# Two transformer layers on one Trainium2 core: six groups of three pairs of feature tiles, with a group's block products between the second products of the group before

## The chip, the core and the metric

The kernel runs on one core of one Trainium2 chip. Its time is the device time in microseconds (us) of one execution of the whole program. Every time quoted here comes from the runs of the kernel before or from one profiled execution of it. In the profile PE is the matrix engine (TensorE), PEld its weight loads, DVE the vector engine, ACT the scalar engine, POOL GpSimd, and SP the sync engine, which in this kernel issues most of the loads.

## The reference

The input is one sequence of 2048 rows of 576 numbers. Two layers follow each other, each of them an attention over eight neighbours at distance two and a feed-forward network with SiLU, both behind a layer norm and a residual sum:

```python
# D = 576, F = 4608, H = 32 heads of 18, window W = 8, dilation 2
x = x + A(layernorm(x), wqkv, wo)
x = x + B(layernorm(x), w1, w2)
x = x + A(layernorm(x), wqkv, wo)
x = x + B(layernorm(x), w1, w2)

def B(x, w1, w2):
    h = silu(x @ w1)          # 2048 x 4608
    return h @ w2             # 2048 x 576
```

A takes, for each row s, the keys and values of the rows s, s-2, ..., s-14 (none before the first row), a softmax over these eight per head, and a projection with wo.

## The kernel before

**Stages.** The 2048 rows are cut into four chunks of 512, and the two layers give eight stages, numbered s = 0 to 7. A stage is the feed-forward network of its chunk, with the attention, the projection and the layer norm of the next stage running beside it on DVE, ACT and POOL and in between on PE (`front`, `attention`, `project`, `forms`). The hidden dimension of 4608 is cut into 36 tiles of 128. float32 values are carried as two fp16 halves, so that each product is made of three matmuls (high by high, high by low, low by high).

**The order.** Nothing is issued as it is written. Each operation goes into a list (`op`, line 79) with an engine, a duration, what it reads and writes and a priority; a small number is urgent. `Plan.order` (line 113) then runs a list schedule: whenever an engine is free in its model, it takes the ready operation of the smallest priority, and among equals the one written first. The result is a fixed order on each engine. On the chip an engine executes its list in order and waits at a semaphore where an operand is not there; everything behind it on that engine waits too.

**Stages 2 to 7** use `ffn_pairs` (line 1068). Two feature tiles and two halves of the chunk make a 2 by 2 block product, which is made from seven block products instead of eight (P1 to P7, lines 1082 to 1108). There are 18 pairs of feature tiles. For each pair:

- Seven weight tiles `wf` (160 KB each, 12 buffers, so 12 block products ahead at most) and two second-weight tiles `w2` (288 KB each, 11 buffers) are loaded by SP (lines 1015 and 856).
- Each of the seven block products is seven matmuls of 128x256 (line 1087) into one of four PSUM banks, called z0, z1, misc0 and misc1.
- ACT copies three of the sums out (L1091), DVE adds three more (L1094), ACT applies SiLU (L1110 to L1114), and ACT and DVE write the two halves of the hidden tile `h` (L1117, L1120; 5 buffers).

The pairs are taken in groups of `G2 = (5, 4, 5, 4)`. When the pairs of a group are through, `second` (line 1128) multiplies them with the second weights: for each of the four row tiles j of the chunk, the n pairs are summed in one of two accumulators `acc` (12 matmuls of 128x288 for each pair, line 1141), and DVE adds the accumulator, scaled, to the residual x (`add_to`, line 848). An `acc` bank can be written again only when DVE has done that. The scales of a group are worked out once, in `tables` (line 946).

All block products and all second products of a stage have the same priority, `pp`, so the order among them is that in which they are written, except that a block product of the next group goes first where a second product is not ready in the model.

**What else stands in the SP queue.** SP also loads the qkv weights of the attention (`wq`, 1080 KB, line 616, one buffer in these stages), x (line 1245), edges of the keys (lines 730 and 731), and issues the transposes for the layer norms (line 459) and for the seven forms of the next stage's input (`xf`, line 1062; 9 buffers, 7 used in a stage). A DMA that waits for a buffer holds all DMAs behind it in the queue.

Of the kernel before, what the change touches and what calls it, by code (L numbers as in the profile page):

```python
# [31 lines left out]
NFT = F // P  # L32
G0 = 6
NB = 2
G1 = 9
# [3 lines left out]
KH = D // 2  # L39
KB = 5 * P  # L40
LNX = 512.0
G2 = (5, 4, 5, 4)
W2N = 11
FAR = 6
PREP = 0.9
# [218 lines left out]
def sliding_attention_silu_ffn(ctx: ExitStack, tc: tile.TileContext, x, wqkv, wo, w1, w2, out):  # L264
    nc = tc.nc
    cp = ctx.enter_context(tc.tile_pool(name="const", bufs=1))
# [4 lines left out]
    op = S.op  # L271

    def fl(t):
        return t.rearrange("p a b -> p (a b)")
# [5 lines left out]
    def T(b):  # L280
        return S.tags[b.tag][b.slot]
# [87 lines left out]
    w2s = [tc.dram_tile([P, 2 * D], F16, name=f"w2s{f}") for f in range(NFT)]  # L369
# [34 lines left out]
    s12 = cp.tile([P, NFT, 2], F32, name="s12")  # L404
# [9 lines left out]
    dz = accw[:, NP:NP + NP // 2, :].rearrange("p a b -> p (a b)")  # L414
    pace = cp.tile([1, 1], F32, name="pace")
    cg = cp.tile([P, NFT // G0], F32, name="cg")
    cg4 = cp.tile([P, 4], F32, name="cg4")
    su = cp.tile([P, NU + 1], F32, name="su")
    ru = cp.tile([P, NU + 1], F32, name="ru")
    du = cp.tile([P, NU], F32, name="du")  # L420
# [43 lines left out]
    PACE_WQ, PACE_WO, PACE_W = (1, 7, 0, 6), (2, 2, 3, 3, 3), (4, 5, 6, 7)  # L464
    gate = []
    formed = []
    highs = []
    turned = []
    marks = []
# [383 lines left out]
        op("SP", 0.38, lambda: nc.sync.dma_start(fl(T(w)), w1s[f]), [("w1s", f)], [w], prio, nbytes=P * 20 * P)  # L853
        return w

    def load_w2(f, prio, kind="w2"):
        w = Buf(kind)
        op("SP", 0.38, lambda: nc.sync.dma_start(fl(T(w)), w2s[f]), [("w2s", f)], [w], prio, nbytes=P * 4 * D)
        return w

    raws = {}
# [84 lines left out]
    def tables():  # L946

        def fn():
            both = s12.rearrange("p f i -> p i f")
            n = 2 * (G2[0] + G2[1])  # L950
            for i, m, cuts in ((1, G1, ((slice(0, 4), slice(0, G1)),)),
                               (2, n, ((slice(0, 4, 2), slice(0, 2 * G2[0])), (slice(1, 4, 2), slice(2 * G2[0], n))))):
                sh, d2 = shs[i], d2s[i]
                nc.vector.scalar_tensor_tensor(sh, both[:, 0], HSH, both[:, 1], op0=ALU.mult, op1=ALU.mult)
                v, r = (t.rearrange("p (g f) -> p g f", f=m) for t in (sh, r12.rearrange("p f i -> p i f")[:, 1]))
                for g, f in cuts:
                    nc.vector.tensor_reduce(cg4[:, g], v[:, :, f], axis=AX.X, op=ALU.min)
                for g, f in cuts:
                    w = f.stop - f.start
                    nc.vector.tensor_tensor(v[:, :, f], r[:, :, f], cg4[:, g, None].to_broadcast([P, NFT // m, w]), op=ALU.mult)  # L960
                nc.vector.reciprocal(d2, cg4)
        op("DVE", 1.9, fn, [("s12", f) for f in range(NFT)], [("sh", i, g) for i in (1, 2) for g in range(4)] + ["cg4"], -0.5)

    def pair_scale():

# [102 lines left out]
    def ffn_pairs(s, xf, xs):  # L1068

        pp, pd = s + 0.5, s - 0.5  # L1070
        q0 = 0
        for g, n in enumerate(G2):
            hb, wbs = [], []
            for q in range(q0, q0 + n):
                wf = {k: load_wf(q, W_ROW[k], pd) for k in P_ORDER}
                w2b = [load_w2(2 * q + f, pd) for f in range(2)]
                c, a, b = Buf("zz"), Buf("zz"), Buf("zz")
                hq, h = Buf("hq" if s >= NC - 1 else "ha"), Buf("hp")
                hb.append(h)
                wbs.append(w2b)  # L1080

                def product(k, z, first, last, wf=wf):
                    def mm():
                        t, w, v = T(z)[:, 0:2 * P], T(wf[k]), T(xf[k])
                        pl = ((0, 0), (3, 0), (0, 3), (1, 1), (4, 1), (1, 4), (2, 2))
                        for m, (u, r) in enumerate(pl):
                            nc.tensor.matmul(t, w[:, u, :], v[:, r, :], start=first and m == 0, stop=m == 6, skip_group_check=True)  # L1087
                    op("PE", 0.763, mm, [wf[k], (xf[k], 0), (xf[k], 1)], [z], pp)

                def snap(z, r, hq=hq):  # L1090
                    op("ACT", 0.32, lambda: nc.scalar.activation(T(hq)[:, r], T(z)[:, 0:2 * P], AF.Copy), [z], [(hq, r)], pd - 0.01)  # L1091

                def add(z, r, hq=hq):
                    op("DVE", 0.36, lambda: nc.vector.tensor_tensor(T(hq)[:, r], T(z)[:, 0:2 * P], T(hq)[:, r], op=ALU.add),  # L1094
                       [z, (hq, r)], [(hq, r)], pd - 0.01)
                product("P5", c, True, False)
                product("P1", a, True, False)
                snap(c, 3)
                snap(a, 0)
                product("P3", c, False, True)  # L1100
                product("P6", a, False, False)
                product("P2", b, True, True)
                snap(a, 1)
                add(b, 0)
                add(c, 1)
                product("P7", a, False, False)
                add(a, 3)
                product("P4", a, False, True)
                d = dz[:, q:q + 1]
                op("ACT", 0.41, lambda a=a, hq=hq, d=d: nc.scalar.activation(T(hq)[:, 2], T(a)[:, 0:2 * P], AF.Silu, scale=d),  # L1110
                   [a, "wsc"], [(hq, 2)], pd - 0.01, table="silu")
                op("ACT", 0.61, lambda hq=hq, d=d: nc.scalar.activation(T(hq)[:, 0:2], T(hq)[:, 0:2], AF.Silu, scale=d),
                   [(hq, 0), (hq, 1), "wsc"], [(hq, 0), (hq, 1)], pd, table="silu")
                op("ACT", 0.41, lambda hq=hq, d=d: nc.scalar.activation(T(hq)[:, 3], T(hq)[:, 3], AF.Silu, scale=d),  # L1114
                   [(hq, 3), "wsc"], [(hq, 3)], pd, table="silu")
                sc = shs[2][:, 2 * q:2 * q + 1]
                op("ACT", 1.08, lambda hq=hq, h=h, sc=sc: nc.scalar.activation(  # L1117
                    T(h)[:, 0].rearrange("p f t -> p (f t)"), T(hq).rearrange("p r t -> p (r t)"), AF.Copy, scale=sc),
                   [(hq, r) for r in range(4)] + [("sh", 2, g)], [(h, 0)], pd)
                op("DVE", 1.2, lambda hq=hq, h=h, sc=sc: nc.vector.scalar_tensor_tensor(  # L1120
                    T(h)[:, 1].rearrange("p f t -> p (f t)"), T(hq).rearrange("p r t -> p (r t)"), sc,
                    T(h)[:, 0].rearrange("p f t -> p (f t)"), op0=ALU.mult, op1=ALU.subtract),
                   [(hq, r) for r in range(4)] + [(h, 0), ("sh", 2, g)], [(h, 1)], pd)
            second(s, g, len(G2), hb, wbs, xs, d2s[2])
            q0 += n
        write_x(s, xs)

    def second(s, g, ng, hb, wbs, xs, d2):

        pp, pd = s + 0.5, s - 0.5  # L1130
        n = len(hb)
        for j in range(NJ):
            acc = Buf("acc")
            last = s == NL * NC - 1 and j == NJ - 1 and g == ng - 1
            for hs_ in ((0,), (1,)) if last else ((0, 1),):
                for t in range(n):
                    def mm2(j=j, acc=acc, t=t, hs_=hs_):
                        for f in range(2):
                            for m, (a, w) in enumerate(((0, 0), (0, 1), (1, 0))):
                                for h in hs_:  # L1140
                                    nc.tensor.matmul(T(acc)[:, h, 0:288], T(hb[t])[:, a, f, j * P:(j + 1) * P],  # L1141
                                                     T(wbs[t][f])[:, w, h * 288:(h + 1) * 288],
                                                     start=t == 0 and f == 0 and m == 0, stop=t == n - 1 and f == 1 and m == 2)
                    op("PE", 0.737 * len(hs_), mm2, [(hb[t], 0), (hb[t], 1)] + wbs[t], [(acc, h) for h in hs_], pp)
                if last:
                    h, = hs_

                    def add_half(j=j, acc=acc, h=h):
                        x_ = T(xs[j])[:, h * 288:(h + 1) * 288]
                        nc.vector.scalar_tensor_tensor(x_, T(acc)[:, h, 0:288], d2[:, g:g + 1], x_, op0=ALU.mult, op1=ALU.add)  # L1150
                    op("DVE", 0.45, add_half, [(acc, h), ("sh", 2, g), xs[j]], [(xs[j], h)], pd)
            if not last:
                op("DVE", 0.75, lambda j=j, acc=acc: add_to(xs[j], acc, d2[:, g:g + 1]),
                   [(acc, 0), (acc, 1), ("sh", 2, g)], [xs[j]], pd)

    def ffn(s, xT, xs):
# [52 lines left out]
        if raw:  # L1209
            tables()  # L1210
            pair_scale()
# [103 lines left out]
```

## Time and profile before

| | us |
|---|---|
| median of three runs | 2183.15 |
| lowest and highest of them | 2179.14, 2187.71 |
| the profiled execution, its own time | 2186.47 |
| its span, first to last instruction | 2184.3 |
| PE busy in the span | 2119.9 |
| DVE busy | 1605.7 |
| ACT busy | 954.5 |
| the six stages of pairs (first block product at 698.4 to the end) | 1485.9 |

A row of the table of groups reads: line, engine, operation, output tile and inputs, partitions by elements and type, count; then the busy time of the group, the mean duration of one in ns, and the idle time of the engine just before them with what ended it. The durations of matmuls overlap, since they are pipelined. What one costs in a row of many is the distance from start to start. A row of a view by windows gives, for a stretch of time, the busy time and the number of instructions of each engine, the granted PE clock (1.00 is full), the busy share of the DMA engines and their rate.

### The profile page before, as it was taken

Reading aid. Unit: us, or ns where it says so; the run is one execution under the profiler, and the core shown is the slowest. Engines: PE = TensorE matmul, PEld = TensorE weight load, DVE = VectorE, ACT = ScalarE, POOL = GpSimd, SP = SyncE. Lnnn points to the kernel's source line nnn. Section 1 sums busy time; section 2 is a strip of 40 time slices with the busy share of each in tenths; the row PEclk is TensorE's granted clock in tenths of the full one; section 3 lists DMA queues with packets and bytes.
Section 4 is the critical chain, followed back from the end, with each engine's and each line's share of the span. In section 5 each row is a group of like instructions: output and inputs, shape, how many; then the busy total and the mean of one; then the engine's idle time right before and its main releaser. Section 6 shows DMA issues by size and latency. Waiting matters only on the chain.

```text
span 2184.3 us, 41276 instructions
## 1 busy us (share of the span) xinstructions
PE 2119.9 (97%) x16198; PEld 1578.8 (72%) x16198; DVE 1605.7 (74%) x2539; ACT 954.5 (44%) x1795; POOL 364.3 (17%) x585
## 2 busy tenths in 40 slices
PE   6999999999999899999999999999999999999999
PEld 3546566656666678876788768887787867888887
DVE  7999998999896897548974599646995569852222
ACT  7545687644344453443324434243433424343232
POOL 2133556234333140001100010000000000000000
PEclk9999999999999999999999999999999999999999
DMA  6476777587879785876539666496655855565443
GB/s 178 149 208 240 244 260 250 176 277 268 194 183 314 229 273 176 197 232 187 165 104 254 164 205 179 111 263 156 203 161 148 237 155 149 160 182 176 140 149 108
DMA packets 334234, 426.19 MB, mean 195 GB/s; under 512 B 145608, under 2 KB 262708, under 8 KB 330072
## 3 DMA queue, kind: packets, MB, share of 16 engines
q1 hardware_dynamic: 292464, 289.10, 47.3%
q0 software_dynamic: 38304, 129.28, 18.3%
q10 hardware_dynamic: 3272, 5.19, 0.9%
q8 instruction: 126, 2.06, 0.4%
q14 instruction: 68, 0.56, 0.1%
HBM read 307.32 MB, written 67.68 MB: 172 GB/s over the span
## 4 chain that ended last, share of the span: by engine, by line
PE 81%; DVE 8%; DMA 7%; ACT 2%; issue 1%; POOL 1%; SPq 0%; ACTq 0%; DVEq 0%
PE acc L1141 25%; PE misc L1087 11%; PE z L1087 11%; PE z L670 8%; PE acc L1202 8%; PE z L1183 7%; PE misc L670 5%; PE acc L841 4%; DMA w<-wfs 3%; DVE lg L773 1%; DVE pr L802 1%; DVE pr L769 1%; DVE pr L809 1%; DMA w<-w2s 1%; DMA wq<-in_B_w_dram 1%
## 5 line engine op out<-in xcount | busy, mean ns | idle before, releaser
L1141 PE MATMUL acc<-w,h 128*128 128x288 f16 x5184 | 653.7, 286 | 2.2 <-DVE h L1120 1.6
L1141 PEld LDWEIGHTS <-h 128*128 128x128 f16 x5184 | 506.5, 98 | 130.4 <-DVE h L1120 1.9
L1087 PEld LDWEIGHTS <-w 128*128 128x128 f16 x5292 | 518.9, 98 | 97.3 <-DMA w<-wfs 21.4
L1087 PE MATMUL z<-xb,w 128*128 128x256 f16 x2653 | 339.2, 275 | 14.0 <-DMA w<-wfs 9.9
L1087 PE MATMUL misc<-xb,w 128*128 128x256 f16 x2639 | 333.9, 273 | 10.4 <-DMA w<-wfs 8.6
L848 DVE SCALAR_TENSOR_TENSOR x<-acc,d,x 128x576 f32<-128x576 f32 x135 | 109.5, 812 | 179.1 <-PE acc L1141 171.2
L670 PEld LDWEIGHTS <-xa 128*128 128x128 f16 x1344 | 132.1, 99 | 116.7 <-issue 9.3
L1202 PE MATMUL acc<-w,h 128*128 128x288 f16 x1728 | 214.6, 286 | 0.0
L1202 PEld LDWEIGHTS <-h 128*128 128x128 f16 x1728 | 168.9, 98 | 43.9
L769 DVE TENSOR_TENSOR pr<-qt,kvs 128x2304 f32<-128x2304 f32 x64 | 163.4, 2553 | 34.6 <-DMA kvs<-kvs 24.7
L802 DVE TENSOR_TENSOR pr<-kvs,pe 128x1152 f32<-128x1152 f32 x128 | 169.9, 1352 | 1.1
L773 DVE TENSOR_REDUCE lg<-pr 128x128 f32<-128x2304 f32 x64 | 163.0, 2547 | 1.1
L809 DVE TENSOR_TENSOR pr<-pr 128x1152 f32<-128x1152 f32 (+1 forms) x128 | 135.2, 1056 | 3.4
L1183 PE MATMUL z<-xb,w 128*128 128x512 f16 x588 | 130.8, 383 | 6.0 <-ACT w L918 2.4
L1120 DVE SCALAR_TENSOR_TENSOR h<-wq,sh,h 128x1024 f16<-128x1024 f32 x60 | 76.9, 1281 | 72.6 <-ACT h L1117 72.6
L670 PE MATMUL z<-wq,xa 128*128 128x432 f16 x588 | 114.1, 350 | 4.2 <-ACT w L683 4.2
L841 PE MATMUL acc<-wo,yo 128*128 128x288 f16 x896 | 115.9, 289 | 2.3 <-DMA yo<-yh 2.2
L670 PE MATMUL misc<-wq,xa 128*128 128x432 f16 x588 | 113.1, 349 | 0.8 <-ACT qt L740 0.8
L1183 PEld LDWEIGHTS <-w 128*128 128x128 f16 x588 | 57.5, 98 | 76.6 <-DVE w L920 2.9
L841 PEld LDWEIGHTS <-yo 128*128 128x128 f16 x896 | 88.1, 99 | 27.1 <-DMA yo<-yh 2.7
L750 POOL DMA_DIRECT2D kvs<-kvs x64 | 33.8, 535 | 374.8 <-ACT qt L740 348.1
L1183 PE MATMUL z<-xb,wq 128*128 128x512 f16 x420 | 93.2, 379 | 0.7 <-ACT hs L1185 0.7
(227 smaller groups left out, 2495.5 us busy)
## 6 DMA issues: line engine op xcount, KB each, us to landing
w<-wfs SPq DMA_DIRECT2D x756, 160.0 KB
w<-w2s SPq DMA_DIRECT2D x252, 288.0 KB
wq<-wqs SPq DMA_DIRECT2D x17, 1080.0 KB
kvs<-kd POOLq DMA_DIRECT2D x8, 1584.0 KB, 8.6
w<-w1s SPq DMA_DIRECT2D x36, 320.0 KB
wfs<-xa POOLq DMA_DIRECT2D x18, 640.0 KB, 4.9
w2s<-w POOLq DMA_DIRECT2D x36, 288.0 KB, 4.1
w1s<-wq POOLq DMA_DIRECT2D x30, 320.0 KB, 4.1
```

Source lines behind the costliest of these rows:

```text
L670: nc.tensor.matmul(T(m)[:, :3 * UC], a, b, start=n == 0, stop=n == len(pl) - 1)
L769: nc.vector.tensor_tensor(T(pr), T(qt)[:, j:j + 2, None, :].to_broadcast([P, 2, W, UC]), win(T(kv), j, 2), op=ALU.mult)
L773: nc.vector.tensor_reduce(T(lg)[:, j:j + 2].rearrange("p a w h -> p (a w h)"), T(pr).rearrange("p a w (h d) -> p (a w h) d", d=DH), axis=A ...
L802: nc.vector.tensor_tensor(T(pr)[:, a].rearrange("p w (h d) -> p w h d", d=DH), v, T(pe)[:, j + a, :, :, None].to_broadcast([P, W, UH, DH]) ...
L809: nc.vector.tensor_tensor(t[:, :, 0:h, :], t[:, :, 0:h, :], t[:, :, h:2 * h, :], op=ALU.add)
L841: nc.tensor.matmul(T(acc)[:, h, 0:288], a, b[:, h * 288:(h + 1) * 288], start=n == 0, stop=n == len(pl) - 1)
L848: nc.vector.scalar_tensor_tensor(t, T(acc)[:, :, 0:288], d, t, op0=ALU.mult, op1=ALU.add)
L1087: nc.tensor.matmul(t, w[:, u, :], v[:, r, :], start=first and m == 0, stop=m == 6, skip_group_check=True)
L1120: op("DVE", 1.2, lambda hq=hq, h=h, sc=sc: nc.vector.scalar_tensor_tensor(T(h)[:, 1].rearrange("p f t -> p (f t)"), T(hq).rearrange("p r t ...
L1141: nc.tensor.matmul(T(acc)[:, h, 0:288], T(hb[t])[:, a, f, j * P:(j + 1) * P], T(wbs[t][f])[:, w, h * 288:(h + 1) * 288], start=t == 0 and ...
L1183: nc.tensor.matmul(T(z), v, u, start=m == 0, stop=m == len(pl) - 1)
L1202: nc.tensor.matmul(T(acc)[:, h, 0:288], T(hb[q])[:, a, j * P:(j + 1) * P], T(wbs[q][0])[:, w, h * 288:(h + 1) * 288], start=q == 0 and m = ...
```

## The change

It does four things. The 18 pairs are cut into six groups of three. A block product of pair q gets the priority `pp + 0.01 q`, and a second product of group g gets `at`: the second products of row tiles j = 0 and 1 stand behind the first pair of group g + 1, those of j = 2 and 3 behind its second pair. The two second weights of a group's third pair are loaded only after the first block product of the group's first pair (`begun`). And `tables` works out scales for six groups of equal size.

```diff
-G2 = (5, 4, 5, 4)
+G2 = (3, 3, 3, 3, 3, 3)
...
-    cg4 = cp.tile([P, 4], F32, name="cg4")
+    cg4 = cp.tile([P, len(G2)], F32, name="cg4")
...
+    begun = []
...
-    def load_w2(f, prio, kind="w2"):
+    def load_w2(f, prio, kind="w2", after=()):
         w = Buf(kind)
-        op("SP", 0.38, lambda: nc.sync.dma_start(fl(T(w)), w2s[f]), [("w2s", f)], [w], prio, nbytes=P * 4 * D)
+        op("SP", 0.38, lambda: nc.sync.dma_start(fl(T(w)), w2s[f]), [("w2s", f)], [w], prio, nbytes=P * 4 * D, after=after)
...
-            n = 2 * (G2[0] + G2[1])
-            for i, m, cuts in ((1, G1, ((slice(0, 4), slice(0, G1)),)),
-                               (2, n, ((slice(0, 4, 2), slice(0, 2 * G2[0])), (slice(1, 4, 2), slice(2 * G2[0], n))))):
+            for i, m in ((1, G1), (2, 2 * G2[0])):
+                n = NFT // m
...
-                for g, f in cuts:
-                    nc.vector.tensor_reduce(cg4[:, g], v[:, :, f], axis=AX.X, op=ALU.min)
-                for g, f in cuts:
-                    w = f.stop - f.start
-                    nc.vector.tensor_tensor(v[:, :, f], r[:, :, f], cg4[:, g, None].to_broadcast([P, NFT // m, w]), op=ALU.mult)
-                nc.vector.reciprocal(d2, cg4)
+                nc.vector.tensor_reduce(cg4[:, :n], v, axis=AX.X, op=ALU.min)
+                nc.vector.tensor_tensor(v, r, cg4[:, :n, None].to_broadcast([P, n, m]), op=ALU.mult)
+                nc.vector.reciprocal(d2, cg4[:, :n])
...
-                w2b = [load_w2(2 * q + f, pd) for f in range(2)]
+                w2b = [load_w2(2 * q + f, pd, after=begun[-2:-1] if q > q0 + 1 else ()) for f in range(2)]
...
-                    op("PE", 0.763, mm, [wf[k], (xf[k], 0), (xf[k], 1)], [z], pp)
+                    return op("PE", 0.763, mm, [wf[k], (xf[k], 0), (xf[k], 1)], [z], pp + 0.01 * q)
...
-                product("P5", c, True, False)
+                begun.append(product("P5", c, True, False))
...
                 for t in range(n):
+                    at = pp + 0.01 * ((g + 1) * n + (j * n + t) // 6) + 0.005
...
-                    op("PE", 0.737 * len(hs_), mm2, [(hb[t], 0), (hb[t], 1)] + wbs[t], [(acc, h) for h in hs_], pp)
+                    op("PE", 0.737 * len(hs_), mm2, [(hb[t], 0), (hb[t], 1)] + wbs[t], [(acc, h) for h in hs_], at)
```

In the changed file the lines stand a little elsewhere: 1087 is 1084, 1141 is 1139, 848 is 849, 858 is 859, 1017 is 1014, 616 is 617, 841 is 842, 1094 is 1091 and 1120 is 1117.

**SP's queue at the start of stage 2.** `w2s_162` to `w2s_170` are the second weights of the tiles 2 to 10, `wfs_197` and `wfs_198` the block weights of the pairs 1 and 2. Before:

```order
L858 DMA w_93<-w2s_162 128x1152
L858 DMA w_93<-w2s_163 128x1152
L858 DMA w_93<-w2s_164 128x1152
L858 DMA w_93<-w2s_165 128x1152
L858 DMA w_93<-w2s_166 128x1152
L858 DMA w_93<-w2s_167 128x1152
L858 DMA w_93<-w2s_168 128x1152
L858 DMA w_93<-w2s_169 128x1152
L858 DMA w_93<-w2s_170 128x1152
L1017 DMA w_70<-wfs_197 128x640 x2
L1017 DMA w_70<-wfs_198 128x640 x7
```

Now:

```order
L859 DMA w_93<-w2s_162 128x1152
L859 DMA w_93<-w2s_163 128x1152
L1014 DMA w_70<-wfs_197 128x640
L859 DMA w_93<-w2s_164 128x1152
L859 DMA w_93<-w2s_165 128x1152
L1014 DMA w_70<-wfs_197 128x640
L859 DMA w_93<-w2s_166 128x1152
L1014 DMA w_70<-wfs_198 128x640
L859 DMA w_93<-w2s_167 128x1152
L1014 DMA w_70<-wfs_198 128x640 x6
```

The last two block weights of pair 1 stood behind nine second weights; now they stand behind two and behind four, and the whole of pair 2 behind six.

**SP's queue in stage 4, round a load of qkv weights** (`wqs_217`, the fourth quarter). Before:

```order
L858 DMA w_93<-w2s_180 128x1152
L1017 DMA w_70<-wfs_202 128x640
L616 DMA wq<-wqs_217 128x4320
L1017 DMA w_70<-wfs_202 128x640
L1017 DMA w_70<-wfs_203 128x640 x7
L1017 DMA w_70<-wfs_204 128x640 x7
L1017 DMA w_70<-wfs_205 128x640 x7
L1017 DMA w_70<-wfs_206 128x640 x2
```

Now:

```order
L1014 DMA w_70<-wfs_204 128x640 x7
L1014 DMA w_70<-wfs_205 128x640 x5
L617 DMA wq<-wqs_217 128x4320
L859 DMA w_93<-w2s_177 128x1152
L859 DMA w_93<-w2s_178 128x1152
L859 DMA w_93<-w2s_179 128x1152
L859 DMA w_93<-w2s_180 128x1152
L859 DMA w_93<-w2s_181 128x1152
L1014 DMA w_70<-wfs_205 128x640 x2
L1014 DMA w_70<-wfs_206 128x640 x7
L1014 DMA w_70<-wfs_207 128x640 x4
```

Before, 24 block weights in a row follow the load of the qkv weights. Now five second weights follow it, and block weights come in runs of some 12 with second weights between the runs. On PE, before, the 24 block products that belong to these rows stand in one run behind the third quarter of this stage's qkv product; now three second products of 12 matmuls and then 12 block products stand behind it, and no run of block products in the middle of a stage is longer than 14.

**DVE's list in stage 7.** L1094 and L1091 are the sums of a pair, L1120 and L1117 write the second half of its `h`, L848 and L849 add an accumulator to x. Before:

```order
L1120 SCALAR_TENSOR_TENSOR h<-hs,sh_267,h 128x1024
L1094 TENSOR_TENSOR wq<-z_101,wq 128x256
L1094 TENSOR_TENSOR wq<-misc_103,wq 128x256
L1094 TENSOR_TENSOR wq<-z_100,wq 128x256
L1120 SCALAR_TENSOR_TENSOR h<-wq,sh_267,h 128x1024
L848 SCALAR_TENSOR_TENSOR x_78<-acc_105,d_270,x_78 128x576
L848 SCALAR_TENSOR_TENSOR x_79<-acc_104,d_270,x_79 128x576
L848 SCALAR_TENSOR_TENSOR x_80<-acc_105,d_270,x_80 128x576
L848 SCALAR_TENSOR_TENSOR x_81<-acc_104,d_270,x_81 128x576
```

Now:

```order
L849 SCALAR_TENSOR_TENSOR x_78<-acc_105,d_270,x_78 128x576
L1117 SCALAR_TENSOR_TENSOR h<-hs,sh_267,h 128x1024
L849 SCALAR_TENSOR_TENSOR x_79<-acc_104,d_270,x_79 128x576
L1091 TENSOR_TENSOR wq<-z_100,wq 128x256
L1091 TENSOR_TENSOR wq<-misc_103,wq 128x256
L1091 TENSOR_TENSOR wq<-z_101,wq 128x256
L1117 SCALAR_TENSOR_TENSOR h<-wq,sh_267,h 128x1024
L849 SCALAR_TENSOR_TENSOR x_80<-acc_105,d_270,x_80 128x576
L849 SCALAR_TENSOR_TENSOR x_81<-acc_104,d_270,x_81 128x576
```

The four additions to x came together behind the last `h` of a group. Now they come in twos between the pairs of the next group, and a stage has 24 of them in place of 16. POOL's list is the same row for row, and PE's is the same up to the twelfth block product of stage 2.

More of the change, by code (lines that the diff above doesn't have):

```diff
@@ L955, in fn @@
                 v, r = (t.rearrange("p (g f) -> p g f", f=m) for t in (sh, r12.rearrange("p f i -> p i f")[:, 1]))
-                for g, f in cuts:
-                    nc.vector.tensor_reduce(cg4[:, g], v[:, :, f], axis=AX.X, op=ALU.min)
-                for g, f in cuts:
-                    w = f.stop - f.start
-                    nc.vector.tensor_tensor(v[:, :, f], r[:, :, f], cg4[:, g, None].to_broadcast([P, NFT // m, w]), op=ALU.mult)
-                nc.vector.reciprocal(d2, cg4)
-        op("DVE", 1.9, fn, [("s12", f) for f in range(NFT)], [("sh", i, g) for i in (1, 2) for g in range(4)] + ["cg4"], -0.5)
+                nc.vector.tensor_reduce(cg4[:, :n], v, axis=AX.X, op=ALU.min)
+                nc.vector.tensor_tensor(v, r, cg4[:, :n, None].to_broadcast([P, n, m]), op=ALU.mult)
+                nc.vector.reciprocal(d2, cg4[:, :n])
+        op("DVE", 1.9, fn, [("s12", f) for f in range(NFT)], [("sh", i, g) for i, m in ((1, G1), (2, 2 * G2[0])) for g in range(NFT // m)] + ["cg4"], -0.5)
     def pair_scale():
@@ L1080, in ffn_pairs, with product @@
                 wbs.append(w2b)
-                def product(k, z, first, last, wf=wf):
+                def product(k, z, first, last, wf=wf, q=q):
                     def mm():
```

## The prediction

> **What bounds the kernel now.** I read the page first, then the stages by windows, then who PE waits for, and then the queue behind those waits.
>
> ```profile
> span 2184.3 us, 41276 instructions
> PE 2119.9 (97%) x16198; PEld 1578.8 (72%) x16198; DVE 1605.7 (74%) x2539; ACT 954.5 (44%) x1795; POOL 364.3 (17%) x585
> ...
> L1141 PE MATMUL acc<-w,h 128*128 128x288 f16 x5184 | 653.7, 286 | 2.2 <-DVE h L1120 1.6
> ...
> L1087 PE MATMUL z<-xb,w 128*128 128x256 f16 x2653 | 339.2, 275 | 14.0 <-DMA w<-wfs 9.9
> L1087 PE MATMUL misc<-xb,w 128*128 128x256 f16 x2639 | 333.9, 273 | 10.4 <-DMA w<-wfs 8.6
> L848 DVE SCALAR_TENSOR_TENSOR x<-acc,d,x 128x576 f32<-128x576 f32 x135 | 109.5, 812 | 179.1 <-PE acc L1141 171.2
> ```
>
> PE is the bound. The second products hardly wait (2.2 us in 5184 matmuls); what PE waits for is block weights. The stages of pairs, in windows from the first block product of a stage to that of the next:
>
> ```profile
> core 0: us, PE busy (x) PEld busy (x) DVE busy (x) ACT busy (x) POOL busy (x), PEclk, DMA share, GB/s
> 698.40:932.10 233.70, 219.61 (x1860) 182.37 (x1858) 175.32 (x269) 98.14 (x183) 41.22 (x60) 0.98 0.79 227
> 932.10:1193.40 261.30, 257.61 (x2085) 203.31 (x2084) 187.09 (x293) 95.71 (x196) 20.21 (x32) 1.00 0.66 182
> 1193.40:1454.50 261.10, 257.74 (x2085) 203.26 (x2083) 186.05 (x290) 95.86 (x196) 16.45 (x28) 1.00 0.66 181
> 1454.50:1716.40 261.90, 259.19 (x2084) 204.06 (x2083) 184.27 (x286) 96.17 (x196) 10.65 (x20) 0.99 0.65 181
> 1716.40:1977.90 261.50, 259.24 (x2085) 204.09 (x2083) 183.14 (x280) 96.34 (x196) 10.64 (x20) 0.99 0.63 174
> 1977.90:2184.30 206.40, 202.41 (x1748) 170.48 (x1745) 57.09 (x90) 67.13 (x126) 0.54 (x1) 1.00 0.45 141
> ```
>
> Length less PE busy is PE's idle time: 14.1 us in stage 2, then 3.7, 3.4, 2.7 and 2.3. The last window's 4.0 is mostly the output behind the last matmul. So 26.2 us is all the idle time that an order of stages 2 to 6 can save. Who ends it, first in stages 3 to 6 (932 to 1978), then in stage 2:
>
> ```profile
> PE misc L1087 <- DMA w<-wfs: 7.0, 5, 2.5
> PE z L1087 <- DMA w<-wfs: 1.5, 1, 1.5
> PE z L1087 <- ACT hs L1091: 0.8, 2, 0.5
> ...
> PE z L1087 <- DMA w<-wfs: 8.4, 1, 8.4
> PE acc L1141 <- DVE h L1120: 1.6, 1, 1.6
> PE misc L1087 <- DMA w<-wfs: 1.5, 1, 1.5
> PE z L1087 <- DVE yo L1094: 1.2, 2, 0.7
> ```
>
> Loads of block weights end 8.5 us in stages 3 to 6, and 8.4 and 1.5 in stage 2. Some of these waits cost more than their length:
>
> ```profile
> 1685.50:1689.00 3.50, 3.50 (x20) 2.46 (x19) 0.42 (x1) 1.50 (x3) 0.00 (x0) 0.53 1.01 186
> 1815.40:1818.60 3.20, 3.16 (x15) 2.24 (x16) 3.20 (x6) 0.99 (x2) 0.00 (x0) 0.51 0.99 316
> 721.00:726.20 5.20, 4.69 (x22) 3.17 (x22) 3.53 (x4) 1.90 (x3) 0.00 (x0) 0.50 1.05 278
> ```
>
> These are stretches right behind three of the waits, with the granted clock at about half: 3.5 x 0.47 + 3.2 x 0.49 + 5.2 x 0.50 = 5.8 us lost beside the idle time. The whole that can be won is 26.2 + 5.8 = 32 us of 2184, or 1.5%. (The Trainium skill, "TensorE: Matmul & The Clock Gate", section "What's actually happening", has the clock halved after an idle window of about 3.4 us. By that only the wait of 8.4 us would be followed by half clock, and 2.6 of the 5.8 us could be won; the rows at 1685 and 1815 have it behind waits of about 2 us, and they decide.)
>
> **Why the loads are late.** In stage 3, PE and SP's queue round one of the waits:
>
> ```profile
> 1020.34 0.93 PE L1087 MATMUL misc<-xb,w 128*128 128x256 f16 x7
> 1020.53 0.32 SPq L616 DMA_DIRECT2D wq<-wqs  x1
> 1021.30 11.64 SPq L1017 DMA_DIRECT2D w<-wfs  x11
> 1028.21 0.93 PE L1087 MATMUL misc<-xb,w 128*128 128x256 f16 x7
> 1031.66 1.70 PE L1087 MATMUL misc<-xb,w 128*128 128x256 f16 x14 [2.52 <-DMA w<-wfs]
> ```
>
> And a stretch behind the next stage's wait of this kind:
>
> ```profile
> 1284.00:1294.00 10.00, 7.54 (x65) 5.97 (x62) 9.72 (x18) 5.57 (x10) 0.62 (x2) 1.00 1.01 294
> ```
>
> The load of qkv weights (L616) waited until PE had read the last ones at 1020.5, and held SP's queue meanwhile. From 1020.34 PE ran block products alone, one every 0.77 us. Twelve `wf` buffers last 12 x 0.767 = 9.2 us, and the next load, issued at 1021.3 behind 1.08 MB, was used at 1031.66, 10.4 us later. So a run of more than about 12 block products behind such a load starves, and the order before has 24 in one run there.
>
> **The change, part by part.** The work of PE is the same: 5292 block matmuls and 5184 second ones. Alternating them costs nothing by these rows of stage 7:
>
> ```profile
> 2154.94 1.63 PE L1141 MATMUL acc<-w,h 128*128 128x288 f16 x12
> 2156.41 0.93 PE L1087 MATMUL z<-xb,w 128*128 128x256 f16 x7
> 2157.17 1.63 PE L1141 MATMUL acc<-w,h 128*128 128x288 f16 x12
> ```
>
> From start to start 12 second matmuls take 1.47 us (0.122 each) and seven block matmuls 0.76 to 0.77 (0.109 each), at the switch too. Everything ahead of stage 2, and stage 7 but for its start, has nothing to win.
>
> *A. Shorter runs of block products in stages 3 to 6.* The 9.2 us of buffers are now stretched by second products, which take no block weights: behind the load of stage 4 stand 3 x 1.47 = 4.4 us of second products and then 12 block products and one second one, so the thirteenth weight is needed 15 us after the qkv product in place of 9.2. It stands behind 1.08 MB and five second weights (2.6 MB in all, 9 us at the 294 GB/s of that stretch), whose buffers come free over those 4.4 us. It should land at 11 to 14 us: cover, but a narrow one. Won at most: 8.5 idle and 3.2 of half clock, 11.7; at least 0. I take 8.5, nearer to the upper end by the 15 us against the 10.4 measured, and in the same way the 1.5 of stage 2.
>
> *B. The start of stage 2.*
>
> ```profile
> 692.71 9.82 SPq L858 DMA_DIRECT2D w<-w2s  x9
> 705.01 18.70 SPq L1017 DMA_DIRECT2D w<-wfs  x12
> 720.89 1.68 PE L1087 MATMUL z<-xb,w 128*128 128x256 f16 x7 [8.42 <-DMA w<-wfs]
> ```
>
> Nine second weights (2.65 MB) went first, and the weight on which PE stood until 720.9 was issued only at 705.0. Now two go first. Its buffer is free after the first block product, 698.4 + 0.9 = 699.3, so it is issued some 5.5 us earlier. Won: 0 if POOL's traffic, which stays as it is, sets its landing; 8.4 + 2.6 = 11.0 if the wait goes. I take the 5.5 by which the issue moves, and none of the half clock.
>
> *C. Second weights of a third pair wait for the group's first block product.* Until the second product that reads them, PE has 20 block products (15 us) and, but for a stage's first group, 12 second ones (18 us) to do, against the 10.4 us that a load took in the worst row above. So I take 0, and nothing can be won. With that cover gone, 1 us of lateness in each of 36 groups would cost 36 us.
>
> *D. 48 more additions to x on DVE*, 24 in place of 16 in each of six stages: 48 x 0.812 = 39.0 us, 6.5 a stage. They lie in DVE's idle time, which is 58 us in stage 2, 74 to 78 in stages 3 to 6 and 149 in stage 7. They can reach PE where DVE runs behind, in the attention:
>
> ```profile
> 1257.84 12.29 PE L1141 MATMUL acc<-w,h 128*128 128x288 f16 x99
> 1273.01 0.81 DVE L848 SCALAR_TENSOR_TENSOR x<-acc,d,x 128x576 f32<-128x576 f32 x1
> ```
>
> A sum that was complete at 1270.1 was taken up at 1273.0 and its bank was free at 1273.8, 3.7 us later. A block of three pairs takes 3 x 1.47 = 4.4 us, and the bank is needed after the other bank's block at the earliest. So it is covered by 0.7 us or by the block products between. Nothing here can save time. Lost: from 0 to 6.5 us in each of the five stages with attention beside them, 32. I take 2, some 0.4 a stage, as block sums wait behind an 0.8 us addition a little more often.
>
> Sum against the profiled execution: -8.5 - 1.5 - 5.5 + 2 = -13.5 us, so 2173.0 from its 2186.5 (span 2184.3 and 2.2 around it). That execution lies 3.3 above the median of 2183.15; from the median it is 2170. This lies 0.6% below, just beyond the 0.5% (11 us) that I count as the least that runs of this kernel, spread over 0.4%, can tell from no change.
>
> **The rivals.**
>
> *1. DVE sets the pace of the attention.* The list puts the additions of the feed-forward network ahead of the attention, so each stage's attention ends later. Counting by the prices above, the last projection (L841) stands 58 us of PE work ahead of the end of stage 4 before, and 39 after. The next stage's input forms must fit there. If this cover is used up, or sums wait behind the attention's operations of 2.5 us, PE takes the 6.5 us in five stages: 32 lost and A's and B's 15.5 won give 2183 + 17 = 2200. For it: DVE is 187 of 261 us busy in stage 3, and 9.72 of 10 in the attention (the row at 1284). Against it: the projections waited for nothing in stages 3 to 6 before, by this row, and 39 us is much.
>
> ```profile
> L841 PE MATMUL acc<-wo,yo 128*128 128x288 f16 x448 | 57.5, 286 | 0.0
> ```
>
> It decides once the attention runs some 20 us later than the list has it, or sums wait longer than a bank's turn.
>
> *2. The waits only move.* The weights come late by another load: five second weights behind the qkv weights, or the 26 block products that begin a stage. Then A is 0 to 4, B some 3, D 2, and the time is 2178 to 2182. For it: DMA shares near 1.0 in the stretches above. Against it: stage 4 began, before, with 33 block products with one second product between, and PE stood nowhere in them:
>
> ```profile
> 1190.00:1215.00 25.00, 25.00 (x226) 21.90 (x225) 13.11 (x39) 10.97 (x22) 0.55 (x1) 1.00 0.91 296
> ```
>
>
> *3. All waits go*, the small ones for ACT and DVE too, since the pairs come at an even pace: 2183 - 32 = 2151.
>
> **How the numbers follow.** My forecast has 0.46, rival 3 0.12, rival 2 0.17, rival 1 0.25. The forecast's own range is 2160 to 2178, so of its 0.46 I count 0.36 as faster by over 0.5% (below 2172) and 0.10 as no change. Faster: 0.36 + 0.12 = 0.48. Within 0.5%: 0.10 + 0.17 = 0.27. Slower: 0.25. The range goes from rival 3 (2151) to near rival 1 (2197), as its loss may be a part of the 6.5 us a stage; some 1 in 10 lies above and less below.
>
> **What would show it.** Right: in windows of stages 3 to 6 PE idle below 2 us each, with no wait for `wf` over 1 us and no half clock; in stage 2 a first wait of some 3 us in place of 8.4; 183 rows of the addition to x with about 39 us more of DVE; stages of about 259 us. Wrong: `wf` waits still behind the qkv loads (A), a first wait of 8 us or more (B), second products waiting for `w2` (C), or PE waiting for DVE's sums, for `acc` or at the projections and at a stage's first block product (D and rival 1).

## The result and the profile after

| | before | changed |
|---|---|---|
| median of seven runs, us | 2181.86 | 2164.63 |
| lowest and highest | 2176.10, 2187.71 | 2161.94, 2176.29 |
| span of the profiled execution | 2184.3 | 2161.5 |

The ratio is 0.9929, with a 95% interval of 0.9906 to 0.9951: the change is faster, by 17 us between the medians. From the page of the changed kernel, the rows that answer to those of before:

```profile
span 2161.5 us, 41247 instructions
...
PE 2111.8 (98%) x16198; PEld 1579.2 (73%) x16198; DVE 1638.9 (76%) x2585; ACT 977.3 (45%) x1803; POOL 364.7 (17%) x585
...
L1139 PE MATMUL acc<-w,h 128*128 128x288 f16 x5184 | 669.5, 286 | 0.6 <-DVE x L1148 0.6
...
L1084 PE MATMUL z<-xb,w 128*128 128x256 f16 x2646 | 334.3, 273 | 9.2 <-DMA w<-wfs 6.5
L1084 PE MATMUL misc<-xb,w 128*128 128x256 f16 x2646 | 337.1, 273 | 0.8 <-DVE yo L1091 0.3
L849 DVE SCALAR_TENSOR_TENSOR x<-acc,d,x 128x576 f32<-128x576 f32 x183 | 148.3, 811 | 140.7 <-PE acc L1139 132.7
```

The matmuls are the same in number. The idle time ahead of the block products fell from 14.0 + 10.4 = 24.4 us to 9.2 + 0.8 = 10.0. The 48 additions to x are there (183 rows for 135) with their 38.8 us of DVE. By stages, in the windows view of the changed kernel (length, then busy time and count of PE, PEld, DVE, ACT and POOL, granted clock, DMA share, GB/s; stages 5 and 6 stand together, since the new order moves work across their border):

```profile
697.30:922.20 224.90, 219.20 (x1860) 182.78 (x1858) 179.23 (x274) 100.17 (x183) 41.28 (x60) 0.98 0.81 233
922.20:1180.90 258.70, 256.89 (x2084) 203.67 (x2082) 191.76 (x298) 100.70 (x198) 20.23 (x32) 1.00 0.65 179
1180.90:1441.60 260.70, 257.36 (x2084) 203.49 (x2082) 191.74 (x299) 100.61 (x198) 16.48 (x28) 1.00 0.68 182
1441.60:1955.10 513.50, 513.50 (x4167) 407.48 (x4166) 379.31 (x588) 200.68 (x396) 21.33 (x40) 1.00 0.67 182
1955.10:2161.50 206.40, 202.44 (x1748) 170.71 (x1745) 64.32 (x98) 70.19 (x126) 0.54 (x1) 1.00 0.47 145
```

Stage 2 is 8.8 us shorter (224.9 for 233.7). Stages 3 to 6 are 12.9 shorter (1032.9 for 1045.8), with PE idle for 1.8 and 3.3 us in stages 3 and 4 and for nothing in 5 and 6. Stage 7 is the same, and 1.1 us lie ahead of stage 2. In stages 3 to 6 the idle time went from 12.0 to 5.2 us and the half clock, 3.2 us, is gone. That makes 10.0. Most of the other 2.9 is a part of the waits that counts as busy: a block matmul is busy for 0.273 us, while in a row the next one starts after 0.109, so a wait delays PE by 0.16 us more than its idle time. The trace has 20 waits in stages 3 to 6 before, very short ones included, and 5 now, which makes 2.5 us. What PE still waits for, from the view of waits in stages 3 to 6 and then in stage 2:

```profile
PE z L1084 <- DVE hs L1091: 2.2, 2, 1.8
PE z L1084 <- DMA w<-wfs: 1.8, 1, 1.8
PE acc L842 <- DVE x L849: 0.9, 1, 0.9
...
PE z L1084 <- DMA w<-wfs: 4.7, 2, 2.9
```

Block weights end 2.1 us of waits in stages 3 to 6 where they ended 8.5 (1.8 here and 0.3 in a row left out), and 4.7 in stage 2 where they ended 9.9.

### The profile page after: what moved, and what is told of

Its sections match the earlier page's. It is cut to its first block, busy times and chain, and to the rows that moved or that the text cites. A ratio compares the mean times of both kernels' runs of the same rounds, so it can differ in the third digit from the quotient of the medians.

```text
span 2161.5 us, 41247 instructions
## 1 busy us (share of the span) xinstructions
PE 2111.8 (98%) x16198; PEld 1579.2 (73%) x16198; DVE 1638.9 (76%) x2585; ACT 977.3 (45%) x1803; POOL 364.7 (17%) x585
## 4 chain that ended last, share of the span: by engine, by line
PE 84%; DMA 6%; DVE 5%; ACT 2%; issue 1%; ACTq 0%; POOL 0%; SPq 0%; DVEq 0%; POOLq 0%
PE acc L1139 28%; PE z L1084 12%; PE misc L1084 12%; PE acc L1200 9%; PE z L1181 8%; PE z L671 6%; PE acc L842 5%; PE misc L671 4%; DMA yo<-yh 2%; DMA w<-wfs 1%; DVE pr L803 1%; DVE pr L810 1%; DMA h<-in_A_wqkv_dram 1%; DMA kvs<-kvs 1%; DVE pr L770 0%
## 5 line engine op out<-in xcount | busy, mean ns | idle before, releaser
L1139 PE MATMUL acc<-w,h 128*128 128x288 f16 x5184 | 669.5, 286 | 0.6 <-DVE x L1148 0.6
L1084 PE MATMUL z<-xb,w 128*128 128x256 f16 x2646 | 334.3, 273 | 9.2 <-DMA w<-wfs 6.5
L849 DVE SCALAR_TENSOR_TENSOR x<-acc,d,x 128x576 f32<-128x576 f32 x183 | 148.3, 811 | 140.7 <-PE acc L1139 132.7
L1200 PE MATMUL acc<-w,h 128*128 128x288 f16 x1728 | 214.6, 286 | 0.0
L1117 DVE SCALAR_TENSOR_TENSOR h<-wq,sh,h 128x1024 f16<-128x1024 f32 x60 | 76.8, 1280 | 71.3 <-ACT h L1114 71.3
L671 PE MATMUL z<-wq,xa 128*128 128x432 f16 x658 | 124.7, 346 | 3.6 <-ACT w L684 3.6
L1088 ACT ACTIVATE wq<-z 128x256 f32<-128x256 f32 x95 | 36.0, 381 | 169.9 <-PE z L1084 169.9
L751 POOL DMA_DIRECT2D kvs<-kvs x64 | 33.9, 536 | 417.0 <-ACT qt L741 384.9
L671 PE MATMUL misc<-wq,xa 128*128 128x432 f16 x518 | 100.8, 350 | 0.8 <-ACT qt L741 0.8
```

Of the source, the lines that this page charges most:

```text
L671: nc.tensor.matmul(T(m)[:, :3 * UC], a, b, start=n == 0, stop=n == len(pl) - 1)
L849: nc.vector.scalar_tensor_tensor(t, T(acc)[:, :, 0:288], d, t, op0=ALU.mult, op1=ALU.add)
L1200: nc.tensor.matmul(T(acc)[:, h, 0:288], T(hb[q])[:, a, j * P:(j + 1) * P], T(wbs[q][0])[:, w, h * 288:(h + 1) * 288], start=q == 0 and m = ...
```

## The experiments

The change has three parts that can be had apart: the groups of three, the interleaving (the priorities of block products and second products), and the held second weights. With both ends, the runs make this table. One corner, groups of three with the held loads and no interleaving, was not run. Each ratio is to the runs of the kernel before on the same chip, whose medians lie between 2181.86 and 2185.60; rows of different chips are compared by the ratios.

| groups | interleaved | held | median, us | ratio to before on the same chip, 95% interval |
|---|---|---|---|---|
| 5, 4, 5, 4 | no | no | 2181.86 | 1 |
| threes | no | no (e1) | 2187.24 | 1.0018 (1.0003 to 1.0032) |
| 5, 4, 5, 4 | no | yes (e4) | 2184.11 | 1.0007 (0.9995 to 1.0020) |
| 5, 4, 5, 4 | yes | no (e3) | 2163.13 | 0.9909 (0.9892 to 0.9926) |
| threes | yes | no (e2) | 2167.19 | 0.9923 (0.9904 to 0.9942) |
| 5, 4, 5, 4 | yes | yes (e10) | 2169.24 | 0.9933 (0.9918 to 0.9949) |
| threes | yes | yes (the change) | 2164.63 | 0.9929 (0.9906 to 0.9951) |

**e1: groups of three alone.**

```diff
-[z], pp + 0.01 * q)
+[z], pp)
...
-[(acc, h) for h in hs_], at)
+[(acc, h) for h in hs_], pp)
...
-w2b = [load_w2(2 * q + f, pd, after=begun[-2:-1] if q > q0 + 1 else ()) for f in range(2)]
+w2b = [load_w2(2 * q + f, pd) for f in range(2)]
```

> The change with its two other parts undone: groups of three pairs, but one priority for all products and no held second weights. Theory (late block weights): at the start of stage 2 nine second weights again stand ahead of the last two block weights of pair 1, so the wait of about 8 us there is back; the runs of block products in the middle of a stage are 12 to 20 long (24 to 34 before, 14 in the change), so a part of A is won. About 2172 to 2178, or 4 to 10 us below before. Rival 'the group size does it': within 3 us of the change, about 2162 to 2168. Rival 'the additions to x cost': since nothing is won and 39 us of DVE are added, 2183 or above.

Measured: 2187.24 us, ratio 1.0018 (1.0003 to 1.0032), a little slower than before. The runs of block products are indeed shorter, and the waits for their weights in stages 3 to 6 fell to some 2 us, but others came. From the view of waits of e1, stages 2 to 6:

```profile
PE z L1084 <- DMA w<-wfs: 9.9, 3, 8.3
PE z L1084 <- DVE hs L1091: 4.1, 4, 1.8
PE z L1084 <- DVE wq L1091: 3.9, 4, 2.6
PE misc L1084 <- DVE hs L1091: 3.7, 4, 1.5
PE acc L1139 <- DVE h L1117: 2.9, 3, 1.6
PE misc L1084 <- DVE wq L1091: 1.4, 4, 0.7
```

DVE's sums (L1091) and hidden tiles (L1117) end 16.0 us of PE's waits in these rows. Before, these two lines ended 4.0 us. So smaller groups without interleaving lose by DVE what they win by DMA; the profiled execution lies 6 us above the median of e1, so its waits are on the high side. Whether the 48 additions or the new order of DVE's list make these waits, this run does not separate. The theory's expectation was too low by 9 us, since it priced only the weights. The time is that of the rival "the additions to x cost", but not for its reason alone: something was won, at the loads, and lost again.

**e2: the change without the held loads.** The last edit of e1 alone.

> The change without the held second weights. Theory: stages 3 to 6 as in the change (PE idle under 4 us in stages 3 and 4 each, near 0 in 5 and 6), the start of stage 2 as before (a wait of about 8 us and half clock behind it): the change plus 5 to 9 us, 2169 to 2174. Rival 'the held loads also smooth stages 3 to 6': waits for block weights there come back too, 2174 to 2182.

Measured: 2167.19 us, ratio 0.9923. From its view of waits in stages 2 to 6:

```profile
PE z L1084 <- DMA w<-wfs: 8.9, 2, 8.3
```

The wait at the start of stage 2 is back at 8.3 us, as the theory has it, but the time is only 2.6 us above the change, where the theory has 5 to 9, and the two intervals overlap.

**e3: the interleaving alone**, on the kernel before.

```diff
-    op("PE", 0.763, mm, [wf[k], (xf[k], 0), (xf[k], 1)], [z], pp)
+    op("PE", 0.763, mm, [wf[k], (xf[k], 0), (xf[k], 1)], [z], pp + 0.01 * q)
...
+    at = pp + 0.01 * (q1 + (j * n + t) // (2 * n)) + 0.005
...
-    op("PE", 0.737 * len(hs_), mm2, [(hb[t], 0), (hb[t], 1)] + wbs[t], [(acc, h) for h in hs_], pp)
+    op("PE", 0.737 * len(hs_), mm2, [(hb[t], 0), (hb[t], 1)] + wbs[t], [(acc, h) for h in hs_], at)
```

Here `q1` is the first pair of the next group.

> The kernel before with the interleaving alone: groups of 5, 4, 5, 4, block products with the priority by pair, the second products of row tiles 0 and 1 behind the next group's first pair and the others behind its second. Runs of block products in the middle of a stage are 12 to 15 long, 23 to 26 at a stage's start. Theory: the waits behind the qkv loads mostly go, the wait at the start of stage 2 stays: 2172 to 2177. Rival 'small groups are needed': no gain, 2180 to 2186.

Measured: 2163.13 us, ratio 0.9909 (0.9892 to 0.9926): as fast as the whole change, without its groups, its 48 additions and its held loads. The windows of e3 by stage:

```profile
699.10:913.90 214.80, 204.33 (x1740) 171.12 (x1738) 171.03 (x259) 97.33 (x179) 39.59 (x57) 0.98 0.78 233
913.90:1185.50 271.60, 271.60 (x2205) 215.41 (x2203) 192.28 (x304) 100.24 (x202) 21.83 (x35) 1.00 0.69 187
1185.50:1442.20 256.70, 256.70 (x2085) 203.74 (x2082) 186.26 (x290) 99.10 (x198) 16.47 (x28) 1.00 0.66 184
1442.20:1699.80 257.60, 256.86 (x2084) 203.70 (x2082) 184.82 (x286) 98.83 (x198) 10.65 (x20) 1.00 0.65 184
1699.80:1956.80 257.00, 256.89 (x2084) 203.71 (x2083) 182.81 (x280) 98.97 (x198) 10.64 (x20) 1.00 0.62 177
```

The first row has 120 matmuls fewer than stage 2 had before and the second 120 more, since the new order moves them over the border. Length less PE busy is 0.0, 0.0, 0.7 and 0.1 us in stages 3 to 6. The only great wait left is the one at the start of stage 2, from the view of waits in stages 2 to 6:

```profile
PE z L1087 <- DMA w<-wfs: 8.3, 1, 8.3
PE acc L1142 <- DVE h L1120: 1.6, 1, 1.6
PE misc L1087 <- DVE hs L1094: 0.7, 1, 0.7
```

 From the first block product of stage 2 to the end of the span e3 takes 2163.3 - 699.1 = 1464.2 us, the change 2161.5 - 697.3 = 1464.2, and before 1485.9. That ends both rivals, "small groups are needed" and "the group size does it". The theory's own range, 2172 to 2177, is missed by 9 us on the good side: it priced the waits behind the qkv loads, and with them went the waits of PE for ACT and DVE, 3.2 us in stages 3 to 6 and 2.0 in stage 2, and the 1.5 us for weights late in stage 2.

**e4: the held loads alone**, on the kernel before (`after=begun[-2:-1] if q > q0 + 1 else ()` in the call of `load_w2`, as in the change).

> The kernel before with the held loads alone: from the third pair of a group on, the two second weights wait for the first block product of the pair two before. SP's queue at the start of stage 2 is then much as in the change; the runs of block products stay 24 to 34 long. Theory: the first wait of stage 2 falls from 8.4 to about 3 to 5 us and its half clock shrinks, stages 3 to 6 stay about as they are: 2173 to 2179. Rival 'it is all in the order of PE': no gain, within 2 us of before.

Measured: 2184.11 us, ratio 1.0007 (0.9995 to 1.0020): nothing won, as the rival "it is all in the order of PE" has it. The first wait of stage 2 fell, but only from 8.4 to 6.2 us, and in the stages behind it PE waited a little more. From the view of waits of e4:

```profile
PE misc L1088 <- DMA w<-wfs: 8.3, 6, 2.6
PE z L1088 <- DMA w<-wfs: 6.5, 2, 6.2
PE z L1088 <- DVE hs L1095: 2.3, 1, 2.3
PE misc L1088 <- DVE hs L1095: 2.2, 3, 1.5
```

**e5 and e6: nine block-weight buffers in place of twelve**, in the kernel before and in the change.

```diff
-    part("wf", W1A, 12, [5, P], F16)
+    part("wf", W1A, 9, [5, P], F16)
```

> The kernel before with 9 block-weight buffers in place of 12. Theory (runs of block products outlast the buffers): 9 x 0.767 = 6.9 us of cover in place of 9.2, so each wait for block weights in stages 2 to 6 grows by some 2.3 us and others appear, with half clock behind them: 15 to 35 us slower than before, 2197 to 2218. Rival 'the buffers do not matter, PE waits for the rate of the DMA engines': within 8 us of before.

> The change with 9 block-weight buffers in place of 12. Theory: second products stand between the block products, so the same loss of cover costs less than in e5: 0 to 12 us over the change, 2165 to 2177, that is under half of the loss of e5. Rival 'buffers do not matter': within 3 us. Rival 'the change lives on its 12 buffers as well': as much as in e5.

Measured: 2218.02 us for e5, ratio 1.0147 (1.0130 to 1.0164), 35 us over the before of the same chip; 2177.71 for e6, ratio 0.9971 (0.9950 to 0.9993), 13 us over the change by the medians, a little beyond the expected 12, and 9 by the ratios. PE's waits for block weights in stages 2 to 6, first of e5, then of e6:

```profile
PE z L1087 <- DMA w<-wfs: 20.3, 9, 5.4
PE misc L1087 <- DMA w<-wfs: 13.3, 7, 4.7
```

```profile
PE z L1084 <- DMA w<-wfs: 8.2, 3, 5.3
PE misc L1084 <- DMA w<-wfs: 7.4, 6, 2.2
```

With three buffers fewer these waits went from 18.4 to 33.6 us in the kernel before, and from 6.8 to 15.6 in the change. (The profiled execution of e5 lies 6 us above its median, that of e6 6 us below.) So the length of the cover sets these waits, and the rival "the buffers do not matter" is out in both kernels. Alternating block products with second products saves buffers: with nine of them the change is still a little faster than the kernel before with twelve.

**e7: e3 with stage 2's second weights held.** `after=begun[-1:] if s == S2 and 0 < q < 5 else ()` in the call of `load_w2`, so that the block weights of pair 1 go ahead of the nine second weights.

> e3 (groups of 5, 4, 5, 4, interleaved) with the second weights of the pairs 1 to 4 held behind the block product of the pair before, in stage 2 alone, so that the block weights of pair 1 go first there. The theory says that the wait at the start of stage 2 (8.5 us and about 2.6 of half clock in e3) is the queue of nine second weights: it falls to 0 to 5 us, and the time to 2152 to 2160. Rival 'the DMA engines are full there whatever the order in the queue': the same sum of waits in stage 2, within 3 us of e3.

Measured: 2164.09 us, ratio 0.9901 (0.9885 to 0.9917), within 1 us of e3: a miss for the theory. Two stretches of stage 2 in e7:

```profile
697.90:720.00 22.10, 15.87 (x118) 12.59 (x116) 13.26 (x12) 6.28 (x13) 12.07 (x17) 0.85 1.04 316
780.00:790.00 10.00, 6.98 (x55) 5.52 (x53) 6.71 (x11) 6.26 (x10) 1.96 (x3) 0.89 1.06 301
```

The first wait fell to 5.8 us, and a wait of 3.0 came at 785. The DMA engines are busy all through in both stretches (share over 1.0, at 316 and 301 GB/s). Here, what goes first in SP's queue chose which load is late, as the rival of e7 has it.

**e8: nine groups of two pairs** (`G2 = (2,) * 9` in the change).

> The change with nine groups of two pairs: 36 additions to x a stage in place of 24, 72 more in all, 58 us more of DVE than in the change; still interleaved and held. Theory: interleaved, the additions are hidden in DVE's idle time; 0 to 8 us over the change, 2165 to 2173. Rival 'DVE sets the pace of the attention': over half of the 58 us in the five stages with attention beside them reach PE, 20 to 45 us over the change, 2185 to 2210.

Measured: 2170.74 us, ratio 0.9935 (0.9920 to 0.9950), 6 us over the change. Against the text of the expectation, no load is held here: only the second weights of a group's third pair are held, and these groups have none. Nine second weights go first again at the start of stage 2, where PE's first wait for block weights is 6.3 us. So the nearer kernel is e2, 4 us below. The additions to x in e8:

```profile
L849 DVE SCALAR_TENSOR_TENSOR x<-acc,d,x 128x576 f32<-128x576 f32 x255 | 206.8, 812 | 155.4 <-PE acc L1139 147.3
```

72 additions more than in the change or in e2, 58.5 us of DVE, of which at most a tenth reached the time. In stages 2 to 6 DVE ends two notable waits of PE, of 1.6 and 0.5 us at the start of stage 2, and e2 has the same two. While the products are interleaved, DVE does not set the pace.

**e9: the loads of qkv weights on POOL's queue**, on the kernel before.

```diff
-        op("SP", 0.4, lambda: nc.sync.dma_start(fl(T(w.bufs[0])), wqs[u]), ...)
+        q = nc.gpsimd if kind == "wz" else nc.sync
+        op("POOL" if kind == "wz" else "SP", ..., lambda: q.dma_start(fl(T(w.bufs[0])), wqs[u]), ...)
```

> The kernel before with the loads of qkv weights of stages 3 to 7 issued by POOL in place of SP; the run of 24 or 25 block products behind the third quarter stays. Two readings of the waits at 1028, 1290 and 1813. 'The queue' (as the prediction tells it: block weights stand behind 1.08 MB in SP's queue): with the load in another queue the block weights no longer stand behind it, and the wait there falls under 0.5 us in at least three of the four stages; 2174 to 2180. 'The engines' (all transfers share the 16 DMA engines): the 1.08 MB still take their share beside the block weights, the waits there stay at 1 to 3 us, and the time within 4 us of before.

Measured: 2200.48 us, ratio 1.0079 (1.0055 to 1.0103), 15 us slower than the before of the same chip: neither reading gave that, but the queue is refuted. Stage 3 of e9, at the place of the prediction's wait at 1028 (issue times on POOL and SP, and PE):

```profile
1022.65 0.58 POOL L617 DMA_DIRECT2D wq<-wqs  x1 [10.31 <-PE z L671]
1022.95 0.93 PE L1088 MATMUL z<-xb,w 128*128 128x256 f16 x7
1023.14 13.27 SPq L1018 DMA_DIRECT2D w<-wfs  x11
1023.24 2.13 POOL L751 DMA_DIRECT2D kvs<-kvs  x4
...
1034.39 2.95 PE L1088 MATMUL misc<-xb,w 128*128 128x256 f16 x13 [4.40 <-DMA w<-wfs]
```

By the semaphores of the trace PE stood here for the second of the block weights issued from 1023.14 on. It was issued at 1023.91, with no load of qkv weights ahead of it in SP's queue, and it landed at 1034.35, 10.4 us later. Before, the weight for which PE stood at this place was issued at 1022.06 and landed at 1031.62, 9.6 us later. PE waited 4.4 us here where it had waited 2.5. The load of 1.08 MB and the copies of keys behind it (L751, 1.0 MB) went on beside the block weights and took their share. The same place in stages 4 to 6 lost 4.4, 3.0 and 3.6 us. That agrees with the Trainium skill, "DMA: Bandwidth & Descriptors", section "Issuing engines are not separate DMA queues", by which transfers run on the same 16 engines and interleave, whichever engine started them.

**e10: e3 with the held loads in all stages.**

> The change with groups of 5, 4, 5, 4 in place of threes: interleaved and held (e3 with the held loads in all stages). If the interleaving alone carries the gain, as e3 and e4 say, this is e3 again: 2160 to 2167, with PE waits outside stage 2 under 3 us in all. If the groups of three carry a part, it is slower than the change: 2168 or above.

Measured: 2169.24 us, ratio 0.9933 (0.9918 to 0.9949), above the upper end of the first reading and within the second. The ratio, though, is that of the change (0.9929), since the kernel before took 2185.60 on this chip, so the groups of three show no gain. From the view of waits of e10, stages 2 to 6:

```profile
PE z L1088 <- DMA w<-wfs: 10.1, 2, 5.2
```

Outside stage 2 the waits are 3 to 4 us, and in stage 2 block weights end 5.2 and 4.9 us. The second of them stands in the middle of stage 2, as in e7, where e3 has none. That the held loads put it there is the likely reading, as nothing else differs from e3; the ratios of the two are 0.0024 apart, and their intervals overlap a little.

## Why the prediction was right

The direction and the main cause hold: PE's waits for block weights, not the second products, were the most of what could be won, and runs of block products shorter than the buffers last won it. The size was forecast low: 13.5 us against 17 by the medians and 22.8 in the profiled pair, whose execution of the kernel before lies 4.6 us above the median of its seven runs. By steps:

- **PE is the bound, and 32 us is the whole that can be won.** Of these 32 us the change took some 18 in the profiled pair: 8.4 of idle time in stage 2, 6.8 in stages 3 to 6 and 3.2 of half clock. The rest of its 22.8 is the 1.1 us ahead of stage 2 and the part of each wait that counts as busy, which the 32 leave out. e3 took all but the start of stage 2.
- **A, shorter runs.** Taken at 8.5 in stages 3 to 6. Waits for block weights fell there by 6.4 us and the half clock by 3.2, so 9.6 by the prediction's own count; the other waits went from 3.5 to 3.1. The 1.5 taken for stage 2 came whole. e3 and e5 show the mechanism, the length of the run against the buffers. Two of the signs for it failed: stage 4 kept 3.3 us of idle time, not below 2, and a wait for weights of 1.8 us at 1301, not below 1. That wait stands at stage 4's load of qkv weights, where the prediction called the cover narrow. It took the thirteenth weight to be needed 15 us after the qkv product and to land after 11 to 14. It was needed at 15.2, and by the trace it landed at 16.9.
- **Why the loads are late** was told half wrong. The prediction has them behind 1.08 MB in SP's queue. e9 shows that the place in the queue is not what counts: the DMA engines are shared, and a load took 9.6 and 10.4 us beside 1.08 MB in the one queue and in the other. (The weight issued at 1021.3, which the prediction reads as the late one, landed at 1028.1; the one that PE stood for was issued at 1022.06.) The prediction also leaves out the copies of keys, 1.0 MB on POOL's queue, issued from 1021.4 on, the last of which landed at 1032.2, in the same stretch. No run takes them away, so how much of the delay is theirs stays open.
- **B, the start of stage 2.** Taken at 5.5. The first wait fell from 8.4 to 2.9, with a second of 1.9 behind it, so 3.7 were won, and the half clock stayed, as was taken. But e4 and e7 show that this is no gain of its own: alone, the held loads bring nothing that can be measured, and in e7 the DMA engines are full in both stretches in which PE waits. Against e2 the change has shorter waits for weights in stage 2, 4.7 us for 8.8, but no time that can be told apart. Rival 2, the waits only move, is right for this part. The rest of stage 2's 8.8 us are its smaller waits, most of which e3 loses too; the 1.6 us for a hidden tile stays in e3.
- **C, held second weights.** Taken at 0; no second product waits for its weights in the view after.
- **D, 48 more additions.** Taken at 2, from 0 to 32. Three waits of 3.1 us in all end with DVE in stages 3 and 4, where DVE had ended 1.2 in stages 3 to 6 before, so the 2 is about right there; the 2.0 us of waits for ACT are gone. e8 prices 72 more at 6 us at the most.
- **Rival 1** did not come in the change. Groups of three without interleaving (e1) come nearest to it, with DVE's lists behind 16 us of waits.
- **Rival 3**, all waits go, came in stages 3 to 6 of e3, with 0.8 us of idle time left, but not in the change.
- **What the prediction did not see** is that one part carries the change. Its term A put the groups and the order together, and e3 has the whole gain from the order alone. The groups of three, which cost the 48 additions, were not needed.

## What to carry to other kernels

Where two kinds of work share an engine and only one of them draws on the DMA engines, alternate them in pieces that are shorter than the load buffers last; here 12 buffers of 0.77 us met runs of 24 pieces, and the order alone gave 0.9%. Before a load is moved in a queue or to another queue, look at the share of the DMA engines in that stretch: where it is full, the move may only make another load late, as in e7 and e9. When a change has several parts, run each alone, since one may carry it all.

## What the runs showed of the hardware

In the traces the granted clock changes in steps: from 650 us on, every stretch at half clock that ends before the program does lasts 3.41 us or two to four times that, and within a trace all begin on one grid of 3.41 us. What counts is how much of one such step PE was idle, and not the length of the wait. Three waits in windows of such steps, two of the kernel before and, behind them, one of the change:

```profile
1026.95:1030.37 3.42, 2.12 (x18) 1.50 (x16) 3.42 (x4) 2.58 (x6) 0.00 (x0) 1.00 1.04 265
1030.37:1033.78 3.41, 2.12 (x20) 1.90 (x21) 2.21 (x6) 0.38 (x1) 0.00 (x0) 1.00 1.05 318
1033.78:1037.19 3.41, 3.41 (x34) 2.97 (x32) 2.51 (x3) 2.47 (x6) 0.77 (x1) 1.00 0.83 259
1682.32:1685.73 3.41, 1.33 (x13) 0.96 (x11) 1.62 (x2) 1.20 (x3) 0.00 (x0) 1.00 0.98 342
1685.73:1689.14 3.41, 3.41 (x18) 2.36 (x17) 0.42 (x1) 1.50 (x3) 0.00 (x0) 0.50 1.00 177
...
1300.52:1303.93 3.41, 1.64 (x15) 1.15 (x14) 2.30 (x3) 1.38 (x3) 0.81 (x1) 1.00 0.85 258
1303.93:1307.34 3.41, 3.41 (x31) 2.77 (x29) 3.08 (x4) 0.51 (x1) 1.05 (x1) 1.00 0.88 271
```

The wait of 2.5 us at 1028 fell into two steps with 1.3 us idle in each, and the clock stayed full. The wait of 2.1 us at 1682 lay in one step, and the next step ran at half clock, which costs half of 3.41, or 1.7 us. At 1812 two waits of 0.5 and 1.5 us lay in one step, with 1.97 us of idle time by the trace, and half clock followed. The wait of 1.8 us of the change lay in one step too, and no half clock followed. In all twelve profiles, from full clock, half clock followed steps with 1.97 us or more of idle time and none with 1.90 or less.

A load of 160 KB took about as long from issue to landing with a load of 1.08 MB ahead of it in its own queue, 9.6 us, as with that load in another one, 10.4 us. Copies of 1.0 MB on POOL's queue shared the DMA engines in both cases.
